# Splitting two-bank PSUM tiles, moving two kinds of copies from ScalarE to VectorE, and loading the first operands in smaller pieces: attention, a dense layer and routed experts on one Trainium2 core

## The chip, the core and the metric

The kernel runs on 1 core of one Trainium2 chip. The time is device microseconds of one execution. Three runs of the kernel before gave 766.39 us (median), 760.68 and 770.97 us. The rows shown below come from one profiled execution.

## What is computed

Everything is float32. Sizes: batch 4, 8 heads of width 64, 512 local and 32 global positions, 2304 tokens of width 512; 8 experts with hidden width 1024.

```python
# attention: a global row sees everything, a local row sees the globals and |i-j| <= 32
out_g = softmax(q_g @ [k_g, k_l].T / 8) @ [v_g, v_l]
out_l = softmax([q_l @ k_g.T, where(|i-j| <= 32, q_l @ k_l.T, -1e9)] / 8) @ [v_g, v_l]
x = concat(out_g, out_l)                      # 2304 x 512
# dense layer
h = x @ w_in                                  # 2304 x 2048
g = h if h >= 1, 0 if h <= -1, else (h + 1)**2 / 4
x = g @ w_out
# routed experts: tokens with x @ w_skip > 0 go to their best expert e
y = softmax(x @ w_gate)[e] * (relu(x @ w1[e]) @ w2[e])
out = x + y                                   # other tokens: out = x
```

## The kernel before, in words

The order of the instructions on every engine is the order of the program text; each engine works its queue off in order, and the framework puts in the waits, from which tile (a named buffer) an instruction reads or writes. Products that need float32 accuracy are done as three products of a high and a low part (`hi` = the value rounded to the matmul's own format, made by ScalarE; `lo` = the rest, by VectorE), so every weight and activation is split in two.

PSUM, the accumulator memory, has eight banks of 128 x 512 float32. `bank(i, name, shape)` (L81) gives a tile with the tag `b<i>`. Before the change the tags b0 and b6 hold tiles of two banks (`(128, 2, 512)`), b2 to b5 one bank each.

**Attention.** 32 steps (`for s in range(ND + 1)`, L440), one for each of 8 groups n (a batch element and half of its heads), two head pairs and two halves of the positions. In step s TensorE transposes the weights of step s (`transposes`, L302, results copied out by ScalarE at L309), makes the scores of a step up to three ahead (`scores`, L256, into an `s` tile; `take` at L208 alternates between two tiles of each kind), and the values of step s-1 (`values`, L319, L326). VectorE adds the mask and takes the maxima (L275), ScalarE does the exponentials (`exps`, L283), GpSimd scales by the reciprocal of the sum (L299) and copies the globals' columns (L315). VectorE copies the values out (L334).

Once per group, `globals_` (L220) does the same for the global rows in six pieces, divided by `yield`: four score matmuls into an `s` tile (L227); a maximum over 544 columns by VectorE (L230) and its multiple (L232); two exponentials by ScalarE (L234, L236); sum, reciprocal and scaling by VectorE (L239 to L244); two times four transposes (L250), each followed by a ScalarE copy to `pgT` (L252). Where the pieces run is written out by hand: `plan(g, ...)` (L409) names half-steps at which `between` (L413) advances the generator, and `mids` (L411, L454) advances it in a step, between that step's `scores` and `softmax`.

The weights `w_in` arrive as float64. `convert` (L88) makes the float32 value and its two parts in five pieces: load; two ScalarE scalings (L94 and L95); two VectorE bit operations (L97, L98); an add (L101); the high part by ScalarE (L104) and the low part by VectorE (L106). Eight of the 32 weight chunks are converted during attention (`plan(convert_in(...))`, L406), the others during the first 13 steps of the dense layer (`conversions`, L178).

**Dense layer.** Five units of up to 512 tokens, 16 steps each (`for m in range(NM)`, L757). A step is `stage1(m)` (L151: 12 matmuls at L158 into `h_ps[m % 2]`), `stage2(m - 1)` (L558: up to 12 matmuls at L565; in the last unit, which has 256 tokens, it trails by two steps), and `middle(m)` (L540), which turns h into g: ScalarE L544 and L545, VectorE L548 (the last reader of the h tile), ScalarE L549, VectorE L552. `h_ps` is the two halves of one two-bank tile `h` (L430). `route` (L489) works out the expert of every token, in five pieces.

**Experts.** Blocks of up to 256 tokens. `mm1(q, f)` (L702) makes one eighth of the hidden layer: 12 matmuls at L709 into `e_ps[f % 2]`, then ScalarE L713 and VectorE L714, its last reader. `e_ps` is the two halves of one two-bank tile `e` (L811). `mm2` (L740, L744) makes the output in the one-bank tiles `z0` and `z1`. In `products` (L877) a block with more than 128 tokens runs eight `mm1`, then `transpose_rows` (L696) of the next block's rows, then 16 `mm2`; `load_rows` (L685) gathers the next block's rows by indirect DMA on GpSimd's queue. A block of at most 128 tokens uses `mm1_few` (L720, L724), one `e` half after the other, and `transpose_few`. The first block is written out by itself (L813, L854): into its `mm1` the routing of the last two token tiles is woven (`hook`, L830), and after piece (6, 3) `choose_order` (L612), some 30 small VectorE instructions, after which the next rows can be looked up. During a block the next expert's weights are loaded (`prefetch`, L847) and split (L679, L680).

**Start.** SP issues the loads in this order (L364 to L371): half of K (400 KB), Q (512 KB), eight pieces of the mask (40 KB each), the other half of K, the identity, V.

Of the kernel before, what the change touches and what calls it, by code (L numbers as in the profile page):

```python
# [47 lines left out]
def tile_kernel(ctx, tc, q, k, v, w_in, w_out, wsg, w1, w2,  # L48
# [36 lines left out]

    def convert(raw, cvt, src, parts):  # L88
        flat = raw.rearrange("p a b -> p (a b)")
        low, high = raw[:, :, 0], raw[:, :, 1]  # L90
        nc.sync.dma_start(out=flat, in_=src.bitcast(I32))
        yield
        t = cvt() if callable(cvt) else cvt
        nc.scalar.activation(out=t.bitcast(F32), in_=high.bitcast(F32), func=AF.Copy, scale=2.0 ** -112)  # L94
        nc.scalar.activation(out=low, in_=low.bitcast(U32), func=AF.Copy, scale=2.0 ** -29)  # L95
        yield
        nc.vector.tensor_scalar(out=high, in0=high, scalar1=-(1 << 31), scalar2=None, op0=ALU.bitwise_and)  # L97
        nc.vector.scalar_tensor_tensor(out=t, in0=t, scalar=3, in1=high, op0=ALU.logical_shift_left,  # L98
                                       op1=ALU.bitwise_or)
        yield  # L100
        nc.vector.tensor_tensor(out=t, in0=t, in1=low, op=ALU.add)  # L101
        yield
        hi, lo = parts()
        nc.scalar.activation(out=hi, in_=t.bitcast(F32), func=AF.Copy)  # L104
        yield
        nc.vector.tensor_tensor(out=lo, in0=t.bitcast(F32), in1=hi.bitcast(F32), op=ALU.subtract)  # L106

    def convert_in(raw, t, f):
        return convert(raw, t, w_in[:, f, :], lambda: (winH[f], winL[f]))

    def convert_out(raw, t, f):
        def parts():
# [76 lines left out]
    with tc.tile_pool(name="att", bufs=1) as a1:  # L189
# [9 lines left out]
        P_a = [wp.tile([128, 2, 2, 2, 256], F32, tag=f"B{6 + i}", name=f"P_a{i}") for i in range(2)]  # L199
        P_b = [P_a[i // 2][:, i % 2] for i in range(4)]  # L200

        s_ps = [bank(6 * i, f"s{i}", (128, 2, 512)) for i in range(2)]
        t_ps = [bank(2 + i, f"t{i}", (128, 2, 2, 2, 64)) for i in range(2)]
        o_ps = [bank(4 + i, f"o{i}") for i in range(2)]
        turn = {"s": 0, "t": 0}
# [13 lines left out]

        def globals_(n):  # L220
            K = K_b[n % 2]
            g = take("s")
            for keys in (True, False):
                for i in range(2):
                    rhs = (K[:, i, 64:64 + NJ * W].rearrange("p (j c) -> p j c", c=W)[:, :, 0:128]
                           if keys else K[:, i, 32:64])
                    nc.tensor.matmul(g[64 * i:64 * i + 64, 0, :] if keys else g[64 * i:64 * i + 64, 1, 0:SG],  # L227
                                     lhsT=K[:, i, NSLOT:NK], rhs=rhs, start=True, stop=True)
            yield
            nc.vector.tensor_reduce(out=stg[:, 0:1], in_=g.rearrange("p b c -> p (b c)")[:, 0:512 + SG], axis=AX.X,  # L230
                                    op=ALU.max)
            nc.vector.tensor_scalar_mul(stg[:, 1:2], stg[:, 0:1], -0.125)  # L232
            yield
            nc.scalar.activation(out=Pg[:, :, 64:192], in_=g[:, 0].rearrange("p (j c) -> p j c", c=128),  # L234
                                 func=AF.Exp, bias=stg[:, 1:2], scale=0.125, accum_out=stg[:, 2:3])
            nc.scalar.activation(out=Pg[:, 0, 32:64], in_=g[:, 1, 0:SG],  # L236
                                 func=AF.Exp, bias=stg[:, 1:2], scale=0.125, accum_out=stg[:, 3:4])
            yield
            nc.vector.scalar_tensor_tensor(out=stg[:, 4:5], in0=stg[:, 2:3], scalar=1e-9, in1=stg[:, 3:4],  # L239
                                           op0=ALU.add, op1=ALU.add)  # L240
            nc.vector.reciprocal(out=stg[:, 5:6], in_=stg[:, 4:5])
            for j in range(NJ):
                x = Pg[:, j, (32 if j == 0 else 64):192]
                nc.vector.tensor_scalar_mul(x, x, stg[:, 5:6])  # L244
            yield
            for half in range(2):
                pt = take("t").rearrange("p h j a c -> p (h j a c)")
                for x in range(4):
                    j, t = 2 * half + x // 2, x % 2
                    nc.tensor.transpose(pt[:, 128 * x:128 * x + 128], Pg[:, j, 128 * t:128 * t + 128], ident)  # L250
                to = pgT[:, 2 * half:2 * half + 2].rearrange("p j t c -> p (j t c)")
                nc.scalar.activation(out=to, in_=pt, func=AF.Copy)  # L252
                yield


        def scores(s):  # L256
            n, i, jp = its[s]
            sp = s_of[s] = take("s")
            for a in range(2):
                for jj in range(2):  # L260
                    j = 2 * jp + jj
                    for h in range(2):
                        p = slice(64 * h, 64 * h + 64)
                        nc.tensor.matmul(sp[64 * jj:64 * jj + 64, h, 256 * a:256 * a + W], lhsT=Q_b[n % 2][p, i, j, :, a],
                                         rhs=K_b[n % 2][p, i, W * j + 96 * a:W * j + 96 * a + W], start=True, stop=True)

        def px(s, h, a):
            return P_b[s % 4][:, h, a, 96 * a:96 * a + W]
# [3 lines left out]
        def reduce_max(s, h, a):  # L272
            jp = its[s][2]
            m = 2 * a + (1 if jp == a else 0)
            nc.vector.tensor_tensor_reduce(  # L275
                out=px(s, h, a), in0=s_of[s][:, h, 256 * a:256 * a + W], in1=mask[:, m, :], scale=-0.125,
                scalar=3e38, op0=ALU.add, op1=ALU.min, accum_out=st_b[s % 4][:, 2 * h + a:2 * h + a + 1])

        def exps(s):
# [81 lines left out]
            yield  # L361
            nc.gpsimd.tensor_copy(out=tri, in_=trif)

        nc.sync.dma_start(out=K_b[0][:, 0], in_=k[0, :, 0])  # L364
        load(Q_b, q, 0)
        lo, up = slice(0, 64), slice(64, 128)
        for p, m, src in ((lo, 1, 1), (up, 1, 0), (lo, 0, 0), (up, 0, 0), (lo, 2, 2), (up, 2, 2), (lo, 3, 2), (up, 3, 3)):
            nc.sync.dma_start(out=mask[p, m], in_=c_mask[p, src])
        nc.sync.dma_start(out=K_b[0][:, 1], in_=k[0, :, 1])
        nc.sync.dma_start(out=ident, in_=c_ident)  # L370
        load(V_b, v, 0)  # L371
        nc.vector.memset(stg, 0.0)
        nc.scalar.activation(out=stg[:, 6:7], in_=stg[:, 7:8], func=AF.Exp)
        nc.gpsimd.memset(Pg, 0.0)
# [28 lines left out]
        for n in range(NG):  # L403
            o = 8 * n
            steps = {0: (0, 9, 11, 12, 13, 14), NG - 1: (-7, 0, 1, 2, 3, 4)}.get(n, (0, 5, 6, 7, 8, 9))
            plan(convert_in(raws[n % 2], cvts[n % 2], n), *(o + x for x in steps))  # L406
            if n + 1 < NG:
                g = globals_(n + 1)
                plan(g, o + 1, o + 1, o + 3)  # L409
                for x in (1, 2, 3):  # L410
                    mids[4 * n + x].append(g)  # L411
        plan(constants(), 2, 5, 6)
        def between(x):  # L413
            n, i8 = divmod(x, 8)
            for g in calls[x]:
                next(g, None)
            if i8 == 4 and 2 <= n < 6:
                split_x(0, [n - 2])

            if x == NS - 13:  # L420

                sp2 = wp.tile([128, 2, 512, 2], I32, tag="B2", name="sp2")
                sp2t = sp2[:, 1].rearrange("p a b -> p (a b)")[:, 0:512]
                sp0 = wp.tile([128, 2, 512, 2], I32, tag="B0", name="sp0")
                plan(convert_out(sp0[:, 0], cvts[0], 0), *(NS - y for y in (11, 7, 6, 5, 4, 3)))
                plan(convert_out(sp2[:, 0], sp2t, 1), *(NS - y for y in (12, 5, 4, 3, 2, 1)))
            if x == NS - 5:
                sp3 = wp.tile([128, 2, 512, 2], I32, tag="B3", name="sp3")
                raws.extend([sp3[:, 0], sp3[:, 1]])
                h2 = bank(0, "h", (128, 2, 512))  # L430
                h_ps.extend([h2[:, i] for i in range(2)])
                conversions(-2)
            if x == NS - 1:
                sp7 = wp.tile([128, 2, 512, 2], I32, tag="B7", name="sp7")
                raws.extend([sp7[:, 0], sp7[:, 1]])
                conversions(-1)
            if NS - 4 <= x < NS:
                stage1(0, [x - NS + 4])

        for s in range(ND + 1):  # L440
# [9 lines left out]
            for r in range(ahead, min(s + AHEAD + 1, ahead + 2, ND + 1)):  # L450
                if r < ND:
                    scores(r)
                if s < ND:
                    for g in mids[s]:  # L454
                        next(g)
                    mids[s] = []
                softmax(r, r - 1)
                if r < ND:
                    exps(r)
                ahead = r + 1  # L460
            if s >= 1:
                values(s - 1)
            if s < ND and i4 == 0 and 1 <= n and n + 1 < NG:
# [344 lines left out]
    hX = [[wp.tile([128, 2, BLK], F32R, tag=f"x{'hl'[hl]}{c}", name=f"h{hl}_{c}") for c in range(4)]  # L808
          for hl in range(2)]
    hH, hL = ([hX[hl][f // 2][:, f % 2, :] for f in range(NEF)] for hl in range(2))  # L810
    e2 = bank(0, "e", (128, 2, 512))  # L811
    e_ps = [e2[:, i] for i in range(2)]
    mm1(0, 0)  # L813
    stage2(NM - 1)
    store(4)
# [278 lines left out]
```

## Time and profile before

| | us |
|---|---|
| three runs: median, lowest, highest | 766.39, 760.68, 770.97 |
| the profiled execution, its own time | 762.76 |
| its span, first to last instruction | 761.1 |
| attention, until about | 142 |
| dense layer, about | 142 to 556 |
| first expert block, about | 554 to 595 |
| other expert blocks, about | 595 to 757 |

The span is what the trace shows; 1.7 us of the execution's own time lie around it. "Busy" is the time in which an engine has an instruction recorded. The engines are PE (TensorE's matmuls), PEld (its weight loads), DVE (VectorE), ACT (ScalarE), POOL (GpSimd) and SP (which only issues transfers). In a timeline or a group, the brackets or the last column name how long the engine sat idle before and which instruction ended that idle time. Ends of matmuls are modelled, so two matmuls in a row overlap in the records; their starts tell the pace.

### The profile page before, as it was taken

The page shows a single profiled execution, that of the slowest core. Times are in us where ns is not written, and L with a number is a line of the kernel's source. Part 1 is how long each engine was busy: PE and PEld are TensorE (multiplying, and loading weights), DVE is VectorE, ACT ScalarE, POOL GpSimd, SP SyncE. Part 2 cuts the span into 40 slices and gives each one's busy share as a digit, 9 for nine tenths or more (in the row PEclk, how much of TensorE's full clock was granted, in tenths as well). Part 3 has the DMA queues.
Part 4 walks back from the last instruction along what each step waited for, and adds up shares of the span by engine and source line. Part 5 has one row for each costly group of instructions (what it writes and reads, how often), then busy time and mean ns, then how long its engine had stood idle before and what let it go on. Part 6 is the DMA issues. An engine that isn't in the chain of part 4 may idle for free. (4 is left out here: it accounts for less than half of the span.)

```text
span 761.1 us, 12203 instructions
## 1 busy us (share of the span) xinstructions
PE 679.2 (89%) x4329; PEld 550.6 (72%) x4329; DVE 377.4 (50%) x1200; ACT 381.2 (50%) x903; POOL 134.3 (18%) x259
## 2 busy tenths in 40 slices
PE   5988888799999999999999999999976786879686
PEld 2666666588778777887778888887865675767574
DVE  3587677769994333243332444255644352222351
ACT  3899898768985333353333444466630241111241
POOL 1656454600000000000000010200022211202211
PEclk9999999999999999999999999999998999999999
DMA  7455443424511100011000231130012604101400
GB/s 271 163 188 217 186 182 139 167 83 139 169 53 42 70 1 1 0 71 42 1 1 1 110 112 56 29 112 29 1 56 82 211 29 152 50 7 57 151 18 23
DMA packets 21229, 66.06 MB, mean 87 GB/s; under 512 B 3675, under 2 KB 4829, under 8 KB 20116
## 3 DMA queue, kind: packets, MB, share of 16 engines
q1 hardware_dynamic: 18260, 58.41, 21.9%
q0 software_dynamic: 2880, 6.58, 2.9%
q8 instruction: 42, 0.69, 0.4%
q14 instruction: 47, 0.39, 0.2%
HBM read 54.95 MB, written 12.43 MB: 89 GB/s over the span
## 5 line engine op out<-in xcount | busy, mean ns | idle before, releaser
L565 PE MATMUL y<-wout,gh 128*128 128x512 f32 x544 | 140.0, 396 | 0.0
L158 PE MATMUL h<-xh,winH 128*128 128x512 f32 (+2 forms) x320 | 120.2, 376 | 7.7 <-DVE tb L548 7.3
L158 PE MATMUL h<-xh,winL 128*128 128x512 f32 (+2 forms) x320 | 115.4, 360 | 0.0
L158 PE MATMUL h<-xl,winH 128*128 128x512 f32 (+2 forms) x320 | 115.1, 360 | 0.0
L565 PEld LDWEIGHTS y<-wout,gh 128*128 128x128 f32 x544 | 99.4, 189 | 20.1 <-issue 1.2
L548 DVE SCALAR_TENSOR_TENSOR tb<-tb,h 128x512 f32<-128x512 f32 (+2 forms) x80 | 48.5, 606 | 119.1 <-ACT tb L545 118.7
L544 ACT ACTIVATE tb<-h,misc 128x512 f32<-128x512 f32 (+2 forms) x80 | 49.7, 622 | 95.1 <-PE h L158 81.3
L531 POOL DMA_INDIRECT table<-ids,slot x17 | 17.4, 1026 | 401.6 <-DVE slot L529 289.3
L709 PE MATMUL e<-yTH,WA 128*128 128x256 f32 x256 | 55.5, 298 | 31.4 <-DVE h L714 30.5
L158 PEld LDWEIGHTS h<-xh,winH 128*128 128x128 f32 x320 | 60.5, 189 | 24.4 <-DVE tb L548 15.7
L565 PE MATMUL y<-wout,gl 128*128 128x512 f32 x272 | 74.9, 390 | 0.0
L299 POOL TENSOR_SCALAR P_a<-P_a,st 128x160 f32<-128x160 f32 x128 | 59.3, 480 | 65.8 <-DVE st L295 57.9
L552 DVE TENSOR_TENSOR gl<-tb,gh 128x512 fp32r<-128x512 f32 (+2 forms) x80 | 48.9, 611 | 42.0 <-ACT gh L549 41.6
L709 PEld LDWEIGHTS e<-yTH,WA 128*128 128x128 f32 x256 | 42.9, 194 | 37.0 <-DVE h L714 35.7
L549 ACT ACTIVATE gh<-tb 128x512 fp32r<-128x512 f32 (+2 forms) x80 | 45.3, 567 | 45.2 <-DVE tb L548 45.2
L713 ACT ACTIVATE h<-e 128x256 fp32r<-128x256 f32 x40 | 15.3, 383 | 102.5 <-PE e L709 73.4
L158 PEld LDWEIGHTS h<-xh,winL 128*128 128x128 f32 x320 | 60.5, 189 | 8.0
L158 PEld LDWEIGHTS h<-xl,winH 128*128 128x128 f32 x320 | 60.6, 189 | 6.9
L565 PEld LDWEIGHTS y<-wout,gl 128*128 128x128 f32 x272 | 51.1, 188 | 11.0
L283 ACT ACTIVATE P_a<-P_a,st 128x160 f32<-128x160 f32 x128 | 53.1, 419 | 9.2 <-DVE st L275 9.1
L744 PE MATMUL z<-WA,h 128*128 128x512 f32 x240 | 57.6, 394 | 0.0
L744 PEld LDWEIGHTS z<-WA,h 128*128 128x128 f32 x240 | 44.6, 189 | 8.9
(208 smaller groups left out, 1086.4 us busy)
## 6 DMA issues: line engine op xcount, KB each, us to landing
xr<-in_w_dram SPq DMA_DIRECT2D x28, 512.0 KB, 6.6
V<-in_v_dram SPq DMA_DIRECT2D x8, 1024.0 KB, 7.6
K<-in_k_dram SPq DMA_DIRECT2D x7, 800.0 KB, 6.6
raw<-in_w_in_dram SPq DMA_DIRECT2D x10, 512.0 KB, 4.6
sp<-in_w_out_dram SPq DMA_DIRECT2D x10, 512.0 KB, 5.3
Q<-in_q_dram SPq DMA_DIRECT2D x8, 512.0 KB, 7.3
ys<-xT SPq DMA_DIRECT2D x15, 256.0 KB, 3.0
out_dram<-xT SPq DMA_DIRECT2D x15, 256.0 KB, 2.8
```

Of the source, the lines that this page charges most:

```text
L158: nc.tensor.matmul(hp, lhsT=lw, rhs=rx[:, 0:n], start=(c == 0 and k == 0), stop=(c == 3 and k == 2))
L283: nc.scalar.activation(out=px(s, h, a), in_=px(s, h, a), func=AF.Exp, bias=st[:, x:x + 1], scale=-1.0, accum_out=st[:, 4 + x:5 + x])
L299: nc.gpsimd.tensor_scalar(out=px(s, h, a), in0=px(s, h, a), scalar1=st[:, x:x + 1], scalar2=1.0, op0=ALU.mult, op1=ALU.mult)
L531: nc.gpsimd.indirect_dma_start(out=table[:, :], out_offset=bass.IndirectOffsetOnAxis(ap=slot[:, 0:1], axis=0), in_=ids[:, i, :], in_offset ...
L544: nc.scalar.activation(out=t, in_=hp, func=AF.Relu, bias=half, scale=0.5)
L548: nc.vector.scalar_tensor_tensor(out=t, in0=t, scalar=1.0, in1=hp, op0=ALU.min, op1=ALU.max)
L549: nc.scalar.activation(out=a, in_=t, func=AF.Copy)
L552: nc.vector.tensor_tensor(out=b_, in0=t, in1=a.bitcast(F32), op=ALU.subtract)
L565: nc.tensor.matmul(y_ps[q], lhsT=(gL if lows else gH)[:, s], rhs=wo(hl, f), start=(f == 0 and hl == 0 and not lows), stop=(f == NF - 1 and ...
L709: nc.tensor.matmul(hp, lhsT=lw, rhs=ry[:, c], start=(n == 0), stop=(n == 11))
L713: nc.scalar.activation(out=hH[f], in_=hp, func=AF.Relu)
L744: nc.tensor.matmul(z_ps[z], lhsT=lh[:, d], rhs=rw, start=(f == 0 and k == 0), stop=(f == NEF - 1 and k == 2))
```

## The change

- The `s0` pair, `h` and `e` tiles become two tiles of one bank each (tags b0 and b1). The second `s` buffer (b6) stays a two-bank tile.
- In `globals_`, the maximum becomes two reductions (512 and 32 columns) and one VectorE instruction that takes the larger and multiplies; the `pgT` copies move from ScalarE to VectorE.
- The six pieces of `globals_` are spread differently: the pieces at half-steps o+1, o+1, o+3 go to o+1, o+3, o+5, and the pieces in `mids` now run behind that step's `softmax` and `exps`.
- For the eight chunks converted during attention, the scaling of the high word (L94) moves from ScalarE to VectorE.
- The first loads: 416 of 800 columns of the first K half, then the whole mask in one piece, then the rest of K, all on SP; the first half of Q on ScalarE's queue, its second half behind V. Two rows of the mask that are equal to others but for a shift are copied by GpSimd.

```diff
-    def convert(raw, cvt, src, parts):
+    def convert(raw, cvt, src, parts, scale_on_vector=False):
...
-        nc.scalar.activation(out=t.bitcast(F32), in_=high.bitcast(F32), func=AF.Copy, scale=2.0 ** -112)
+        if scale_on_vector:
+            nc.vector.tensor_scalar_mul(t.bitcast(F32), high.bitcast(F32), 2.0 ** -112)
+        else:
+            nc.scalar.activation(out=t.bitcast(F32), in_=high.bitcast(F32), func=AF.Copy, scale=2.0 ** -112)
...
-        s_ps = [bank(6 * i, f"s{i}", (128, 2, 512)) for i in range(2)]
+        s6 = bank(6, "s6", (128, 2, 512))
+        s_ps = [[bank(i, f"s{i}") for i in range(2)], [s6[:, i] for i in range(2)]]
...
-            nc.vector.tensor_reduce(out=stg[:, 0:1], in_=g.rearrange("p b c -> p (b c)")[:, 0:512 + SG], axis=AX.X,
-                                    op=ALU.max)
-            nc.vector.tensor_scalar_mul(stg[:, 1:2], stg[:, 0:1], -0.125)
+            nc.vector.tensor_reduce(out=stg[:, 0:1], in_=g, axis=AX.X, op=ALU.max)
+            nc.vector.tensor_reduce(out=stg[:, 1:2], in_=g32[:, 0:SG], axis=AX.X, op=ALU.max)
+            nc.vector.tensor_scalar(out=stg[:, 1:2], in0=stg[:, 0:1], scalar1=stg[:, 1:2], scalar2=-0.125, op0=ALU.max,
+                                    op1=ALU.mult)
...
-                nc.scalar.activation(out=to, in_=pt, func=AF.Copy)
+                nc.vector.tensor_copy(out=to, in_=pt)
...
-        nc.sync.dma_start(out=K_b[0][:, 0], in_=k[0, :, 0])
-        load(Q_b, q, 0)
-        lo, up = slice(0, 64), slice(64, 128)
-        for p, m, src in ((lo, 1, 1), (up, 1, 0), (lo, 0, 0), (up, 0, 0), (lo, 2, 2), (up, 2, 2), (lo, 3, 2), (up, 3, 3)):
-            nc.sync.dma_start(out=mask[p, m], in_=c_mask[p, src])
+        first_keys = 2 * W + 96
+        nc.sync.dma_start(out=K_b[0][:, 0, 0:first_keys], in_=k[0, :, 0, 0:first_keys])
+        nc.scalar.dma_start(out=Q_b[0][:, 0], in_=q[0, :, 0])
+        nc.sync.dma_start(out=mask, in_=c_mask)
+        nc.sync.dma_start(out=K_b[0][:, 0, first_keys:NK], in_=k[0, :, 0, first_keys:NK])
         nc.sync.dma_start(out=K_b[0][:, 1], in_=k[0, :, 1])
         nc.sync.dma_start(out=ident, in_=c_ident)
         load(V_b, v, 0)
+        nc.sync.dma_start(out=Q_b[0][:, 1], in_=q[0, :, 1])
+
+        nc.gpsimd.tensor_copy(out=mask[64:128, 1], in_=mask[64:128, 0])
+        nc.gpsimd.tensor_copy(out=mask[0:64, 3], in_=mask[0:64, 2])
...
-            plan(convert_in(raws[n % 2], cvts[n % 2], n), *(o + x for x in steps))
+            plan(convert_in(raws[n % 2], cvts[n % 2], n, True), *(o + x for x in steps))
...
-                plan(g, o + 1, o + 1, o + 3)
+                plan(g, o + 1, o + 3, o + 5)
...
-                h2 = bank(0, "h", (128, 2, 512))
-                h_ps.extend([h2[:, i] for i in range(2)])
+                h_ps.extend([bank(i, f"h{i}") for i in range(2)])
...
-                if s < ND:
-                    for g in mids[s]:
-                        next(g)
-                    mids[s] = []
                 softmax(r, r - 1)
                 if r < ND:
                     exps(r)
                 ahead = r + 1
+            if s < ND:
+                for g in mids[s]:
+                    next(g)
...
-    e2 = bank(0, "e", (128, 2, 512))
-    e_ps = [e2[:, i] for i in range(2)]
+    e_ps = [bank(i, f"e{i}") for i in range(2)]
```

## Rows read from the trace of the kernel before

**Rows 1.** The page: busy time of each engine; granted TensorE clock in 40 slices, tenths.

```profile
PE 679.2 (89%) x4329; PEld 550.6 (72%) x4329; DVE 377.4 (50%) x1200; ACT 381.2 (50%) x903; POOL 134.3 (18%) x259
...
PEclk9999999999999999999999999999998999999999
```

**Rows 2.** Busy time by stretch: bounds, length, each engine's busy time, clock, DMA.

```profile
core 0: us, PE busy (x) PEld busy (x) DVE busy (x) ACT busy (x) POOL busy (x), PEclk, DMA share, GB/s
18.00:142.00 124.00, 108.68 (x1304) 83.25 (x1303) 87.95 (x428) 111.86 (x374) 71.46 (x183) 0.96 0.50 182
...
600.00:640.00 40.00, 30.35 (x190) 26.21 (x188) 17.85 (x33) 13.22 (x29) 6.61 (x9) 1.00 0.44 145
```

**Rows 3.** Waits over the whole span: waiter <- releaser: us in total, times, longest.

```profile
PEld e L709 <- DVE h L714: 46.3, 33, 6.2
...
PE e L709 <- DVE h L714: 39.6, 33, 6.1
...
PEld h L158 <- DVE tb L548: 15.7, 33, 2.7
...
PE t L250 <- ACT PT L309: 12.6, 13, 2.1
```

**Rows 4.** Timeline of one expert step: start us, us, instruction, count, idle before.

```profile
601.12 0.39 PE L709 MATMUL e<-yTH,WA 128*128 128x256 f32 x1 [0.93 <-DVE h L714]
...
602.53 0.28 PE L709 MATMUL e<-yTH,WA 128*128 128x256 f32 x1
...
603.27 0.42 DVE L714 SCALAR_TENSOR_TENSOR h<-e,h 128x256 fp32r<-128x256 f32 x1 [1.41 <-ACT h L713]
...
603.75 0.39 PE L709 MATMUL e<-yTH,WA 128*128 128x256 f32 x1 [0.93 <-DVE h L714]
```

**Rows 5.** Groups by line: shapes, count | busy us, mean ns | idle before, releasers.

```profile
L744 PE MATMUL z<-WA,h 128*128 128x512 f32 x240 | 57.6, 394 | 0.0
...
L252 ACT ACTIVATE pgT<-t 128x512 f32<-128x512 f32 x16 | 9.6, 598 | 4.0 <-PE t L250 4.0
...
L94 ACT ACTIVATE cvt<-raw 128x512 f32<-128x512 f32 x12 | 7.9, 657 | 0.0
...
L230 DVE TENSOR_REDUCE stg<-s 128x1 f32<-128x544 f32 x8 | 5.8, 723 | 6.3 <-PE s L227 6.3
...
L572 DVE COPY xT<-y 128x512 f32<-128x512 f32 x8 | 5.1, 681 | 0.0
```

**Rows 6.** Timeline around the end of the first expert block.

```profile
579.95 0.40 DVE L714 SCALAR_TENSOR_TENSOR h<-e,h 128x256 fp32r<-128x256 f32 x1
...
580.41 0.58 PE L709 MATMUL e<-yTH,WA 128*128 128x256 f32 x1 [6.12 <-DVE h L714]
...
583.51 1.01 POOL L687 DMA_INDIRECT nyg<-ys,nid  x1 [0.30 <-PE e L709]
...
593.12 0.59 PEld L698 LDWEIGHTS p<-ident,nyg 128*128 128x128 f32 x4
```

**Rows 7.** Transfers from 585 to 650 us: issues, count, median us to landing.

```profile
nyg<-ys,nid POOLq DMA_INDIRECT x4, 5.5
```

**Rows 8.** Timeline: the second expert's block, and a block of few rows.

```profile
694.49 0.50 PE L724 MATMUL e<-WA,yTH 128*128 128x512 f32 x1 [0.74 <-ACT hr L727]
...
709.17 0.69 DVE L889 COPY cyg<-nyg 128x1024 f32<-128x1024 f32 x1 [3.60 <-DMA out_dram<-ob,pid]
...
710.25 0.58 PE L709 MATMUL e<-yTH,WB 128*128 128x256 f32 x1 [3.52 <-DVE h L714]
```

**Rows 9.** Timeline of the start: first score matmuls, first matmuls of the globals.

```profile
6.04 1.34 PE L264 MATMUL s<-K,Q 64*64 64x160 f32 x16 [6.04 <-DMA Q<-in_q_dram]
...
10.46 2.13 PE L227 MATMUL s<-K 128*64 128x512 f32 x6 [1.18 <-DMA K<-in_k_dram]
```

**Rows 10.** Line 97 alone, ns min/median/max: up to 142 us, and from 160 to 235.

```profile
L97 DVE TENSOR_SCALAR raw<-raw x8: 426/477/509, 40.9 to 137.6; 128x512 int32<-128x512 int32 x8
...
L97 DVE TENSOR_SCALAR raw<-raw x8: 419/421/423, 166.2 to 227.2; 128x512 int32<-128x512 int32 x8
```

More of the change, by code (lines that the diff above doesn't have):

```diff
@@ L106, in convert, with convert_in @@
         nc.vector.tensor_tensor(out=lo, in0=t.bitcast(F32), in1=hi.bitcast(F32), op=ALU.subtract)
-    def convert_in(raw, t, f):
-        return convert(raw, t, w_in[:, f, :], lambda: (winH[f], winL[f]))
+    def convert_in(raw, t, f, scale_on_vector=False):
+        return convert(raw, t, w_in[:, f, :], lambda: (winH[f], winL[f]), scale_on_vector)
     def convert_out(raw, t, f):
@@ L221, in globals_ @@
             K = K_b[n % 2]
-            g = take("s")
+            g, g32 = take("s")
             for keys in (True, False):
@@ L226, in globals_ @@
                            if keys else K[:, i, 32:64])
-                    nc.tensor.matmul(g[64 * i:64 * i + 64, 0, :] if keys else g[64 * i:64 * i + 64, 1, 0:SG],
+                    nc.tensor.matmul(g[64 * i:64 * i + 64, :] if keys else g32[64 * i:64 * i + 64, 0:SG],
                                      lhsT=K[:, i, NSLOT:NK], rhs=rhs, start=True, stop=True)
             yield
-            nc.vector.tensor_reduce(out=stg[:, 0:1], in_=g.rearrange("p b c -> p (b c)")[:, 0:512 + SG], axis=AX.X,
-                                    op=ALU.max)
-            nc.vector.tensor_scalar_mul(stg[:, 1:2], stg[:, 0:1], -0.125)
+            nc.vector.tensor_reduce(out=stg[:, 0:1], in_=g, axis=AX.X, op=ALU.max)
+            nc.vector.tensor_reduce(out=stg[:, 1:2], in_=g32[:, 0:SG], axis=AX.X, op=ALU.max)
+            nc.vector.tensor_scalar(out=stg[:, 1:2], in0=stg[:, 0:1], scalar1=stg[:, 1:2], scalar2=-0.125, op0=ALU.max,
+                                    op1=ALU.mult)
             yield
-            nc.scalar.activation(out=Pg[:, :, 64:192], in_=g[:, 0].rearrange("p (j c) -> p j c", c=128),
+            nc.scalar.activation(out=Pg[:, :, 64:192], in_=g.rearrange("p (j c) -> p j c", c=128),
                                  func=AF.Exp, bias=stg[:, 1:2], scale=0.125, accum_out=stg[:, 2:3])
-            nc.scalar.activation(out=Pg[:, 0, 32:64], in_=g[:, 1, 0:SG],
+            nc.scalar.activation(out=Pg[:, 0, 32:64], in_=g32[:, 0:SG],
                                  func=AF.Exp, bias=stg[:, 1:2], scale=0.125, accum_out=stg[:, 3:4])
@@ L263, in scores @@
                         p = slice(64 * h, 64 * h + 64)
-                        nc.tensor.matmul(sp[64 * jj:64 * jj + 64, h, 256 * a:256 * a + W], lhsT=Q_b[n % 2][p, i, j, :, a],
+                        nc.tensor.matmul(sp[h][64 * jj:64 * jj + 64, 256 * a:256 * a + W], lhsT=Q_b[n % 2][p, i, j, :, a],
                                          rhs=K_b[n % 2][p, i, W * j + 96 * a:W * j + 96 * a + W], start=True, stop=True)
@@ L275, in reduce_max @@
             nc.vector.tensor_tensor_reduce(
-                out=px(s, h, a), in0=s_of[s][:, h, 256 * a:256 * a + W], in1=mask[:, m, :], scale=-0.125,
+                out=px(s, h, a), in0=s_of[s][h][:, 256 * a:256 * a + W], in1=mask[:, m, :], scale=-0.125,
                 scalar=3e38, op0=ALU.add, op1=ALU.min, accum_out=st_b[s % 4][:, 2 * h + a:2 * h + a + 1])
```

## The prediction

> **What bounds the kernel now.** I read the page's engine shares first: TensorE is busy 89% of the span and its clock is granted nearly everywhere, so only its idle time and what it waits for can be won [rows 1]. The busy time by stretch then parts the kernel. In attention it is ScalarE that has least room: 111.86 of 124.00 us, with TensorE at 108.68 and VectorE at 87.95. In the expert stretch no engine is full: TensorE 30.35 of 40.00 us, VectorE and ScalarE below half [rows 2]. There something makes TensorE wait, and the list of waits names it: 33 times the first matmul of `mm1` waits for VectorE's L714, 39.6 us in all. The same pattern, weaker, stands between the dense layer's L158 and L548: 15.7 us on the weight loads [rows 3].
>
> The timeline of one expert step shows why this wait looks needless. The matmuls that start at 603.75 write the half of `e` that was last read two pieces ago, yet they start only when the L714 that began at 603.27, which reads the other half, is done [rows 4]. `mm2` alternates between the one-bank tiles `z0` and `z1` in the same way and has no idle time before it at all [rows 5]. So the wait goes by tile, not by bank, and a one-bank tile should have it two pieces back.
>
> All sums are made against the profiled execution, 762.8 us (span 761.1 and 1.7 around it); the median of the three runs is 3.6 higher.
>
> **The experts' tiles.** A piece goes from 601.12 to 603.75: 2.63 us. Its twelve matmuls start within 601.12 to 602.53, and at that pace (0.118 us each when they run densely) twelve take 1.42. So a wait costs 1.20 us though only 0.93 is shown as idle: 0.27 more, since the tail of the last matmul and the exposed weight load count as busy [rows 4]. For 33 waits that is 39.6 + 33 x 0.27 = 48.5 us [rows 3]. Without the wait, piece f needs the L714 of piece f-2: the last matmul of f-2 starts 1.2 us before that L714 is over (602.53 to 603.27 + 0.42), one dense piece covers 1.42, so nothing is left in the steady part.
>
> What is late next, taken off:
> - First block. The 6.12 us before 580.41 is piece 7 waiting for an L714 queued behind `choose_order` [rows 6]. Piece 7 will run at once, then 20 products of `mm2` (512 columns, so about 0.236 each by the pace above) before the low part from that L714 is needed: 1.42 + 4.7 = 6.1 us of work for a wait of 6.12 + 0.27. What remains with the instruction itself I take as 1 us.
> - The gather for the next rows is issued at 583.51, its transposes run at 593.12, 9.6 us later [rows 6]. It hangs on `choose_order`, which moves forward only by the five or six waits ahead of it, while TensorE gains 5 us more: some 4.6 us are left for a landing that takes 5.5 in the median [rows 7]. 1 us.
> - Second expert's block: the L714 of its first piece is queued behind the copy L889, which starts at 709.17. TensorE now waits 3.52 us before piece 1; it will run piece 1 (1.42) and wait before piece 2 instead: 2.2 us remain [rows 8]. About 0.7 of the same kind in the block before.
>
> 48.5 - 5 = 43.5. In the two blocks of few rows, `mm1_few`'s second half waits 0.74 us for L727, which reads the first [rows 8]: 2 x (0.74 + 0.27) = 2.0. Together 45; bounds 25 (see the first rival) and 50.
>
> **The dense layer's tiles.** 33 waits, 15.7 us on the weight loads, the longest 2.7 [rows 3]. Next late is `stage2`, which needs the g of one step before and comes 12 matmuls after; in the last unit it trails by two steps. I take 12 us of the 15.7, as part of a weight load's idle time is covered by the matmul before; bounds 6 (half the steps find another wait) and 16.
>
> **Attention.** Off ScalarE inside the 18 to 142 us stretch: 14 copies L252 x 0.598 = 8.4 us and 8 scalings L94 x 0.657 = 5.3 us [rows 5]. Onto VectorE: 14 copies of 128x512 out of PSUM, by the nearest row L572 x 0.681 = 9.5; 8 scalings, between L97 in the same pattern (0.464 with POOL busy) and L94's own 0.657, I take 0.47: 3.8 [rows 5, 10]. The split maximum costs less than one of 0.723 per group twice over; by L230's pace I take 0.2 each, 1.6 in all (bounds 0 and 0.72 x 8 = 5.8) [rows 5]. So ScalarE goes from 111.9 to 98, VectorE from 88 to 103, TensorE stays at 108.7 [rows 2]. TensorE is then the longest, and at most 124 - 108.7 = 15 us can go. TensorE waits 12.6 us at the globals' transposes for ScalarE's L309, 13 times [rows 3]. The first four of each group move behind `values`, so half of that goes; the second four still follow the same step's L309. Against it: the `s` tile that the globals hold is given back half a step later, and between two `softmax` on VectorE there now stand normalising, scaling and a copy. With three engines within 10% of each other in fixed order, I take 6 us, bounds -6 and +13.
>
> A rule of the Trainium skill speaks against the moved scaling. First the row: L97, which reads and writes the same strided pattern, takes 0.477 us in the median beside a busy POOL and 0.421 where POOL has no work, 0.06 more [rows 10]. The skill ("SBUF — State Buffer", Who interferes with whom) says that a VectorE `tensor_scalar` may hold the port pair it shares with GpSimd for the whole instruction, the other fully blocking, while ScalarE never waits. Eight blocks of a whole GpSimd instruction would make some 3 us (an estimate from that page), the row only 0.5. I go by the row; the rest of the sum doesn't use this.
>
> **The start.** Ahead of the first scores 400 + 512 KB are asked for now; later 208 + 256 on two queues, the mask beside them. First scores at 6.04; in proportion to the bytes 3 us earlier. But the next stop is the second half of K, waited for until 10.46 [rows 9]: ahead of and with it 1632 KB now, 1376 later, in proportion 1.6 us earlier, and more because it is no longer issued behind eight mask loads. Then TensorE itself (1.34 of scores, the globals) is in the way. 2.5 us; bounds 0 (mask copies on POOL or a transfer on ScalarE's queue late) and 4.
>
> **Sum.** 45 + 12 + 6 + 2.5 = 65.5; 762.8 - 65.5 = 697.3. For runs that lie somewhat above the profiled execution, as here, I forecast 699 us; its own range is 685 to 713.
>
> **The rivals.**
> - *The next rows or weights bind the blocks.* Without stalls a block shrinks by some 8 us, but the gather still waits for the block's ids, and lands after 5.5 us [rows 7]. For it: the chain through POOL is as long as ever. Against: in the stretch 600 to 640 DMA is at 0.44 and all engines have room [rows 2]. If four blocks each lose 4 us and the first 4 more, 45 becomes 25: 719 us.
> - *VectorE becomes attention's bound.* Its 15 us come between the reductions that ScalarE waits for. For: 103 of 124 in fixed order. Against: TensorE still has more. Attention then loses 6 instead of winning 6: 711 us.
> - *The split does nothing*: the waits for L714 and L548 have another reason. Against it stands `z` [rows 5]. Without 45 and 12: 756 us.
> - *Slower: TensorE's clock in attention.* The clock was granted at 0.96 there [rows 2]. Should the new waits (for VectorE's copy out of the two transpose tiles) be long in every step, TensorE would run at the 1.2 GHz level instead of 2.4; all of its 108.7 us would then double. It decides from about 60 us of work at the low level, which eats all that the rest gains; at 75 us: 699 + 6 + 75 = 780. Against: in the worst stretch now the loss is a few per cent.
>
> **How the numbers follow.** Forecast 0.66, rows or weights 0.16, VectorE 0.12, no effect 0.04, clock 0.02. About 2% (15 us) can be told from no change. The first three are faster by more: 0.94; no effect lies within: 0.04; the clock is slower: 0.02. The range takes in the first two rivals and the bounds of attention and dense layer: 683 to 722.
>
> **What would show it.** Right: waits of L709 for L714 fall from 33 to a handful, one wide block's eight pieces take about 11.5 us; no wait of L158 for L548; TensorE busy over 95% in 600 to 640's work; attention shorter by some 6 us with ScalarE no longer fullest. Wrong: L709 waits for L714 as often as before, or transposes L698 wait for the gather, or attention gets longer with VectorE above 90%.

## The result and the profile after

| | before | after |
|---|---|---|
| median of four runs each, side by side (us) | 763.53 | 712.0 |
| lowest and highest | 759.88, 770.97 | 711.7, 716.04 |
| ratio, 95% interval | | 0.9326, 0.9241 to 0.941 |
| profiled execution, its span | 762.76, 761.1 | 711.86, 710.1 |
| first scores start | 6.04 | 4.60 |
| last value matmul starts | 149.6 | 156.9 |
| first expert matmul starts | 554.3 | 547.4 |

The last three rows cut the span into parts. The dense layer (from the last value matmul to the first expert matmul) went from 404.7 to 390.5 us: 14.2 gained. The experts (from there to the end) went from 206.8 to 162.7: 44.1 gained. Attention ends 7.3 us *later*, although it begins earlier. So the kernel is faster by about 51 us, and without attention it would have been more.

All line numbers from here on are those of the changed kernel: `mm1`'s matmul L717 and its last reader L722 (before L709, L714), dense L161 and L556 (L158, L548), scores L269 (L264), globals' transposes L255 (L250), their copy L257 (L252), the weights' copy L314 (L309), values L331 (L326).

The page's busy shares and granted clock, to be held against [rows 1]:

```profile
PE 665.7 (94%) x4329; PEld 547.3 (77%) x4329; DVE 389.9 (55%) x1232; ACT 371.6 (52%) x879; POOL 134.7 (19%) x261
...
PEclk9999999999999999999999999999999999999998
```

Busy time by stretch, as in [rows 2]: attention, the dense layer alone, and 40 us of the experts (bounds, length, PE, PEld, DVE, ACT, POOL, clock, DMA):

```profile
18.00:142.00 124.00, 102.42 (x1219) 76.92 (x1212) 92.53 (x435) 95.96 (x331) 65.42 (x173) 0.97 0.43 161
...
157.00:545.00 388.00, 387.94 (x1986) 321.09 (x1983) 203.02 (x535) 209.97 (x393) 18.14 (x18) 1.00 0.16 55
...
600.00:640.00 40.00, 40.00 (x277) 37.32 (x276) 13.24 (x28) 8.37 (x20) 8.83 (x10) 1.00 0.29 100
```

TensorE is now busy without a gap in the dense layer and in the expert stretch, where [rows 2] had 30.35 of 40 (the stretch is the same in time, not in work, as the blocks come earlier). In attention it does *less* in the same 124 us than before, 102.42 against 108.68, and no other engine has taken its place as the full one.

What L717 waited for, from the view of that one line (us, times). The view adds up matmuls and weight loads; [rows 3] had 39.6 us for the one and 46.3 for the other, 33 times each. Of the 1.0 us left, 0.3 are the matmuls':

```profile
  issue: 7.1, 8
  DVE h L722: 1.0, 3
```

The timeline of the first blocks, to be read against [rows 4] and [rows 6]: the end of the first block's `mm1`, the transposes of the gathered rows, three pieces of the next block by their last reader, and the two idle times of `mm1` at the start of the second expert's block, to be read against [rows 8].

```profile
568.24 4.60 PE L752 MATMUL z<-WA,h 128*128 128x512 f32 x19 [0.39 <-DVE h L722]
...
573.22 0.66 PE L706 MATMUL p<-ident,nyg 128*128 128x128 f32 x4 [0.39 <-DMA nyg<-ys,nid]
...
581.04 0.42 DVE L722 SCALAR_TENSOR_TENSOR h<-e,h 128x256 fp32r<-128x256 f32 x1 [0.23 <-ACT h L721]
...
582.48 0.42 DVE L722 SCALAR_TENSOR_TENSOR h<-e,h 128x256 fp32r<-128x256 f32 x1 [0.23 <-ACT h L721]
...
583.92 0.42 DVE L722 SCALAR_TENSOR_TENSOR h<-e,h 128x256 fp32r<-128x256 f32 x1 [0.23 <-ACT h L721]
...
663.85 0.28 PE L717 MATMUL e<-yTH,WB 128*128 128x256 f32 x1 [1.73 <-issue]
...
666.07 0.39 PE L717 MATMUL e<-yTH,WB 128*128 128x256 f32 x1 [0.27 <-DVE h L722]
```

A piece now comes every 1.44 us, where it took 2.63. L722 is no faster than L714 was: it just has a whole piece of time before its tile is written again. What was to be late next is late by 0.39 us in two of the places named, the end of the first block's `mm1` and the gather; in the second expert's block, where 2.2 us before piece 2 were foreseen, 0.27 are left there, and TensorE idles 1.73 us within piece 0, with no cause that the profile names.

### The profile page after: what moved, and what is told of

It is laid out like the page before. It is cut to its first block, busy times and chain, and to the rows that moved or that the text cites. A ratio compares the mean times of both kernels' runs of the same rounds, so it can differ in the third digit from the quotient of the medians.

```text
span 710.1 us, 12156 instructions
## 1 busy us (share of the span) xinstructions
PE 665.7 (94%) x4329; PEld 547.3 (77%) x4329; DVE 389.9 (55%) x1232; ACT 371.6 (52%) x879; POOL 134.7 (19%) x261
## 5 line engine op out<-in xcount | busy, mean ns | idle before, releaser
L161 PE MATMUL h<-xh,winH 128*128 128x512 f32 (+2 forms) x320 | 118.2, 369 | 0.0
L161 PE MATMUL h<-xh,winL 128*128 128x512 f32 (+2 forms) x320 | 114.6, 358 | 0.0
L161 PE MATMUL h<-xl,winH 128*128 128x512 f32 (+2 forms) x320 | 114.3, 357 | 0.0
L556 DVE SCALAR_TENSOR_TENSOR tb<-tb,h 128x512 f32<-128x512 f32 (+2 forms) x80 | 48.5, 607 | 105.4 <-ACT tb L553 104.9
L304 POOL TENSOR_SCALAR P_a<-P_a,st 128x160 f32<-128x160 f32 x128 | 60.5, 489 | 67.7 <-DVE st L300 61.4
L161 PEld LDWEIGHTS h<-xh,winH 128*128 128x128 f32 x320 | 60.2, 188 | 10.2 <-issue 2.1
L161 PEld LDWEIGHTS h<-xh,winL 128*128 128x128 f32 x320 | 60.2, 188 | 7.8
L161 PEld LDWEIGHTS h<-xl,winH 128*128 128x128 f32 x320 | 60.3, 189 | 7.3
L280 DVE CUSTOM_DVE_ANT_0 P_a<-s,mask 128x160 f32<-128x160 f32 x128 | 37.5, 314 | 27.3 <-PE s L269 18.9
L717 PE MATMUL e<-yTH,WA 128*128 128x256 f32 x256 | 48.7, 286 | 0.8 <-issue 0.7
L553 ACT ACTIVATE tb<-tb 128x512 f32<-128x512 f32 (+2 forms) x80 | 45.5, 568 | 2.5
```

The lines of the kernel that those rows point to most:

```text
L161: nc.tensor.matmul(hp, lhsT=lw, rhs=rx[:, 0:n], start=(c == 0 and k == 0), stop=(c == 3 and k == 2))
L280: nc.vector.tensor_tensor_reduce(out=px(s, h, a), in0=s_of[s][h][:, 256 * a:256 * a + W], in1=mask[:, m, :], scale=-0.125, scalar=3e38, op ...
L304: nc.gpsimd.tensor_scalar(out=px(s, h, a), in0=px(s, h, a), scalar1=st[:, x:x + 1], scalar2=1.0, op0=ALU.mult, op1=ALU.mult)
L553: nc.scalar.activation(out=t, in_=t, func=AF.Square)
L556: nc.vector.scalar_tensor_tensor(out=t, in0=t, scalar=1.0, in1=hp, op0=ALU.min, op1=ALU.max)
L717: nc.tensor.matmul(hp, lhsT=lw, rhs=ry[:, c], start=(n == 0), stop=(n == 11))
```

## Attention: the new wait

The list of waits between 18 and 150 us (waiter <- releaser: us in total, times, longest):

```profile
DVE P_a L280 <- PE s L269: 18.4, 17, 2.8
...
PEld t L255 <- ACT P_a L288: 12.6, 7, 2.3
...
PE t L255 <- DVE Pg L249: 10.8, 7, 2.0
DVE xl L142 <- ACT xh L141: 8.8, 4, 2.2
```

The old wait of the globals' transposes for ScalarE's copies, 12.6 us in [rows 3], is gone. In its place they wait for L249, VectorE's normalising of the globals' weights, once per group (the row of the weight loads, 12.6 us, is the same seven stalls). The timeline of one such step shows how that comes about:

```profile
57.39 0.69 DVE L234 TENSOR_REDUCE stg<-s 128x1 f32<-128x512 f32 x1
...
58.46 0.69 ACT L239 ACTIVATE Pg<-s,stg 128x512 f32<-128x512 f32 x1
...
59.29 1.04 PE L269 MATMUL s<-K,Q 64*64 64x160 f32 x16 [0.82 <-ACT Pg L239]
...
60.26 1.31 PE L331 MATMUL o<-PT,V 128*64 128x160 f32 x16
60.36 0.65 ACT L141 ACTIVATE xh<-xT 128x512 fp32r<-128x512 f32 x1
61.03 0.69 DVE L142 TENSOR_TENSOR xl<-xT,xh 128x512 fp32r<-128x512 f32 x1 [2.21 <-ACT xh L141]
61.64 0.32 DVE L280 CUSTOM_DVE_ANT_0 P_a<-s,mask 128x160 f32<-128x160 f32 x1
...
63.14 1.02 DVE L249 TENSOR_SCALAR Pg<-Pg,stg 128x160 f32<-128x160 f32 x4
...
63.59 0.63 PE L255 MATMUL t<-ident,Pg 128*128 128x128 f32 x4 [2.02 <-DVE Pg L249]
```

Read it from the end. The transposes at 63.59 wait 2.02 us for L249, which began at 63.14. L249 stands in VectorE's queue behind the whole `softmax` of its step (L280, from 61.64). That one is late twice over. Its scores could start only at 59.29, when the globals' exponential L239 had read the `s` tile that the globals held; they were done by 60.33. And ahead of it in VectorE's queue stands L142, the low part of a piece of the dense layer's input, which waits 2.21 us for its high part: L141 is in ScalarE's queue behind the same exponential and the weights' copies L314, and runs from 60.36. `softmax` starts as L142 ends.

L142 runs in four of the groups only. In these four the transposes wait 2.02 us each for L249; in the other three they wait 0.89 to 0.93, as here, one group earlier:

```profile
45.58 0.63 PE L255 MATMUL t<-ident,Pg 128*128 128x128 f32 x4 [0.93 <-DVE Pg L249]
```

While all this runs, the next values wait: they start at 67.05, as the starts of the value matmuls in the group of the step at 59.29 show:

```profile
49.03 1.31 PE L331 MATMUL o<-PT,V 128*64 128x160 f32 x16
52.23 1.31 PE L331 MATMUL o<-PT,V 128*64 128x160 f32 x16
56.14 1.31 PE L331 MATMUL o<-PT,V 128*64 128x160 f32 x16
...
67.05 1.31 PE L331 MATMUL o<-PT,V 128*64 128x160 f32 x16
```

The four steps take 18.02 us (49.03 to 67.05; the start at 60.26 is in the timeline above). The same group before:

```profile
49.48 1.31 PE L326 MATMUL o<-PT,V 128*64 128x160 f32 x16
...
60.31 1.31 PE L326 MATMUL o<-PT,V 128*64 128x160 f32 x16
65.66 1.31 PE L326 MATMUL o<-PT,V 128*64 128x160 f32 x16
```

That is 16.18. The last of the four steps took 5.35 (60.31 to 65.66) and takes 6.79 now. Reckoned from the start of each group's last value matmuls to the next group's, which gives 16.18 and 17.8 here, four of the seven groups grew by 1.6 us each, the four with L142; of the other three one grew by 1.1 and two by nothing. With 2.1 us in the first group that is 9.7 us, against 2.4 won at the start.

## The experiments

Two theories stood after that. *Spacing*: the new half-steps put normalising directly ahead of its transposes, with only a step's values between, and let the globals hold an `s` tile longer. *VectorE*: the copies and scalings moved there are what makes everything late. The first four runs part them. Ratios are to the kernel before on the same chip (median 764.99 us in the first four runs, 765.92 in the second four). The changed kernel itself was timed only beside the 763.53 of the first table; differences to it are between medians of separate comparisons.

**plan_back**: the changed kernel with one line put back.

```diff
-                plan(g, o + 1, o + 3, o + 5)
+                plan(g, o + 1, o + 1, o + 3)
```

> The changed kernel with one line undone: the pieces of globals_ run at half-steps o+1, o+1, o+3 again (still behind softmax), so normalising comes half a step earlier than the transposes that need it. Theory S (the new spacing costs attention its time: TensorE waits for L249, 10.8 us, and for the globals' exponentials, 8.2 us, in the changed kernel's trace): 701 to 704 us, the wait of L255 for L249 below 2 us in all. Rival V (VectorE has too much to do because of the copies and scalings): 709 to 712 us.

Measured: 702.38 us, ratio 0.9193 (0.9124 to 0.9263), 9.6 us below the changed kernel by the medians (the two intervals overlap by 0.002, the runs' ranges lie 8 us apart); in the profiled execution the last value matmul starts at 146.5, 10.4 us earlier. Its waits in attention:

```profile
ACT P_a L288 <- DVE st L280: 16.8, 22, 1.8
DVE stg L244 <- ACT Pg L241: 12.1, 7, 1.9
...
DVE P_a L280 <- PE s L269: 5.3, 10, 1.2
```

L255 no longer waits for L249 at all, L142 no longer for L141, and `softmax` waits 5.3 us for its scores instead of 18.4. The pieces meet their data: VectorE waits for the exponentials' sums (L244) where TensorE used to wait for VectorE. One line explains what attention lost. Some 3 of the 10.4 us are two falls of the granted clock, which this execution does not have (last section); the line moves maximum, exponentials and normalising at once, and no run parts them.

**copy_back**: the changed kernel with the `pgT` copies on ScalarE again.

```diff
-                nc.vector.tensor_copy(out=to, in_=pt)
+                nc.scalar.activation(out=to, in_=pt, func=AF.Copy)
```

> The changed kernel with the pgT copies on ScalarE again, everything else as changed. Theory S: 710 to 714 us, the waits of L255 for L249 stay. Rival V: 703 to 706 us, VectorE's 9 us less on the path.

Measured: 720.46 us, ratio 0.9434 (0.9364 to 0.9505): 8 us *slower* than the changed kernel by the medians, with intervals that overlap a little, and above both theories' ranges. The profiled executions differ by 5.8 us: 2.2 lie in attention (last value matmul 159.1), 3.6 in the experts, whose code is the same; why those are longer stays open.

```profile
DVE P_a L280 <- PE s L269: 28.0, 21, 2.0
...
PE t L255 <- DVE Pg L249: 10.8, 7, 2.0
```

The new wait is the same to the tenth. Taking the copies off VectorE makes attention no shorter, so their move is not what made it longer; with the new spacing it is rather worth those 2.2 us.

**scale_back**: the changed kernel with the eight scalings on ScalarE again.

```diff
-            plan(convert_in(raws[n % 2], cvts[n % 2], n, True), *(o + x for x in steps))
+            plan(convert_in(raws[n % 2], cvts[n % 2], n), *(o + x for x in steps))
```

> The changed kernel with the scaling of the high word on ScalarE again in attention. Theory S: 710 to 714 us. Rival V: 708 to 710 us, by the 3.5 us of VectorE's work.

Measured: 710.8 us, ratio 0.9305 (0.9236 to 0.9374), 1.2 us below the changed kernel and inside its interval. The wait for L249 stays at 10.8 us. With copy_back this ends the VectorE theory: neither move, put back, makes the kernel faster by what that theory asked.

**tiles_only**: the kernel before with nothing but the one-bank tiles and the split maximum that they need.

```diff
-        s_ps = [bank(6 * i, f"s{i}", (128, 2, 512)) for i in range(2)]
+        s6 = bank(6, "s6", (128, 2, 512))
+        s_ps = [[bank(i, f"s{i}") for i in range(2)], [s6[:, i] for i in range(2)]]
...
-                h2 = bank(0, "h", (128, 2, 512))
-                h_ps.extend([h2[:, i] for i in range(2)])
+                h_ps.extend([bank(i, f"h{i}") for i in range(2)])
...
-    e2 = bank(0, "e", (128, 2, 512))
-    e_ps = [e2[:, i] for i in range(2)]
+    e_ps = [bank(i, f"e{i}") for i in range(2)]
```

> The kernel before with nothing but the one-bank tiles (s0 pair, h, e, and the split maximum that the tiles need). If the dense layer and the experts gained by the tiles alone (14.1 and 44.1 us between the traces) and attention lost by the rest: 58 us less than before, 704 to 706 us, attention ending within 1 us of before. If attention's loss came from the split tiles or the second maximum: 711 to 715 us.

Measured: 703.31 us, ratio 0.9197 (0.9127 to 0.9268). This is a little below the 704 to 706 expected of the tiles. They alone are worth 61.7 us; everything else in the change takes back 8.7. In attention the wait of [rows 3] is there as before (this kernel's L252 and L311 are L250 and L309), though the last value matmul comes 2.7 us earlier than in the kernel before, some 1.5 of them one fall of the clock less. In the second expert's block piece 2 waits as the prediction has it:

```profile
PE t L252 <- ACT PT L311: 12.2, 12, 2.0
...
656.95 0.39 PE L710 MATMUL e<-yTH,WB 128*128 128x256 f32 x1 [2.20 <-DVE h L715]
```

The next four runs ask what the remaining parts are worth once the spacing is right, and whether a better kernel than both can be had.

**sched_back**: the changed kernel with the whole old order of the globals' pieces: plan_back's line, and the pieces in `mids` ahead of `softmax` again.

```diff
-                plan(g, o + 1, o + 3, o + 5)
+                plan(g, o + 1, o + 1, o + 3)
...
+                if s < ND:
+                    for g in mids[s]:
+                        next(g)
+                    mids[s] = []
                 softmax(r, r - 1)
...
-            if s < ND:
-                for g in mids[s]:
-                    next(g)
```

> The changed kernel with the whole old schedule of globals_ (half-steps o+1, o+1, o+3, and the other pieces between scores and softmax again); the copies and the scaling stay on VectorE. If only the spacing of the pieces cost time: 701 to 704 us, as with the half-steps alone put back (702.4). If running them behind softmax is worth something by itself (the copies on VectorE then stand ahead of the reductions that ScalarE waits for): 705 to 710 us.

Measured: 698.26 us, ratio 0.912 (0.9024 to 0.9216), wholly below the changed kernel's interval: 13.7 us by the medians, and below both ranges expected. Its waits, and its busy time in the stretch of [rows 2], come from two views:

```profile
ACT P_a L288 <- DVE st L280: 22.1, 15, 2.1
...
PE t L255 <- ACT PT L314: 13.1, 14, 2.2
```

```profile
18.00:142.00 124.00, 108.63 (x1311) 82.29 (x1304) 102.64 (x461) 100.46 (x353) 78.62 (x187) 0.99 0.49 178
```

With the order undisturbed, ScalarE has lost 11.4 us and VectorE has taken 14.7 (against 111.86 and 87.95 before), and yet TensorE waits as long for L314 as it did for L309. A group takes 16.28 us, as before the change.

**tiles_start**: tiles_only with the new first loads.

```diff
-        nc.sync.dma_start(out=K_b[0][:, 0], in_=k[0, :, 0])
-        load(Q_b, q, 0)
...
+        first_keys = 2 * W + 96
+        nc.sync.dma_start(out=K_b[0][:, 0, 0:first_keys], in_=k[0, :, 0, 0:first_keys])
+        nc.scalar.dma_start(out=Q_b[0][:, 0], in_=q[0, :, 0])
...
```

> The kernel before with the one-bank tiles and the new first loads, attention's schedule and copies as before. The first loads brought step 2's scores 2.6 us earlier in the changed kernel's trace. If that carries through: 700 to 701.5 us against 703.3 with the tiles alone. If attention takes it back because ScalarE is its bound: 703 us. Against 702.4 with all of the change but the half-steps, this also says what the moved copies and the scaling are worth: nothing if 702, a loss if below.

Measured: 700.72 us, ratio 0.9131 (0.9037 to 0.9225), 2.6 us below tiles_only by the medians, with intervals that overlap. It differs from sched_back by the copies and scalings alone, which stay on ScalarE here: 700.72 against 698.26, no difference that these runs can tell. In the profiled executions attention even ends 3.4 us earlier here (the last value matmul starts at 143.3 against 146.7); what puts sched_back's execution ahead lies in the experts, whose code is the same (159.6 against 164.3 us).

**norm_late**: the changed kernel with the plan of plan_back, but normalising one half-step later than there: still ahead of its step's `softmax`, and with more time for the globals' exponentials that it needs.

```diff
-                plan(g, o + 1, o + 3, o + 5)
+                plan(g, o + 1, o + 1, o + 4)
```

> The changed kernel with the half-steps o+1, o+1, o+4: matrix products and maximum in one go as before the change, the normalising one half-step later than before it. With o+3 VectorE waits 12.1 us there for the globals' exponentials (L244 for L241). If that wait is on the path: 694 to 699 us. If VectorE would have waited for the next scores anyway: 701 to 703 us.

Measured: 702.38 us, ratio 0.9172 (0.9089 to 0.9255): the same as plan_back. What is left at the transposes is a wait of the weight loads, and some 1 us of the matmuls':

```profile
DVE stg L244 <- ACT Pg L241: 8.7, 6, 1.5
...
PEld t L255 <- ACT PT L314: 4.9, 13, 0.8
```

So both waits at L255, the old one for L314 and the new one for L249, can be all but removed, and the time does not fall below that of sched_back, which keeps 13.1 us of one of them.

**all_banks**: norm_late with the other two-bank tiles split too (the second `s` buffer, the routing's and the small blocks' tiles).

```diff
-        s6 = bank(6, "s6", (128, 2, 512))
-        s_ps = [[bank(i, f"s{i}") for i in range(2)], [s6[:, i] for i in range(2)]]
+        s_ps = [[bank(i, f"s{i}") for i in (6 * k, 6 * k + 1)] for k in range(2)]
...
-    r_ps = bank(6, "r", (128, 2, 512))
+    r_ps = [bank(6 + i, f"r{i}") for i in range(2)]
...
-    f_ps = bank(6, "f", (128, 2, 4, 128))
+    f_ps = [bank(6 + i, f"f{i}", (128, 4, 128)) for i in range(2)]
```

> As the kernel with o+1, o+1, o+4, and the three other two-bank tiles (the second s buffer, r of the routing, f of the short blocks) in one-bank tiles too. If every two-bank tile costs waits like e and h did: 2 to 5 us less than that kernel, above all in the routing steps of the first expert block and the last unit. If these tiles were never waited for across banks: within 1 us of it.

Measured: 701.05 us, ratio 0.9151 (0.9067 to 0.9234), not to be told from norm_late. Of the tiles split here only the `s` buffer showed a wait that went by the tile, and a small one: the scores' wait for the globals' exponentials goes from 7.7 to 6.8 us. Splitting paid where a long wait went by the tile.

## Why the prediction was right, and where it was wrong

The time forecast was 699 us; 712.0 lies in the range and at the upper edge of the likeliest case's own. The 13 us between are one term: attention came out 15.7 us worse than forecast, outside its own bounds of -6 and +13, and the other three terms together 1.2 better. That the total still lay in the range is the range's width, which took in the rivals, and not this term.

- **Experts: 45 predicted, 44.1 measured.** The wait is by tile, it goes with the split, and a piece falls from 2.63 to 1.44 us where 1.42 was worked out. Of the 5 us that were to stay, the 1 us at the first block and the 1 us at the gather came out at 0.39 each, while the 2.2 before piece 2 of the second expert's block came as foreseen in tiles_only (2.2) and tiles_start (2.1); the changed kernel has 1.73 us within piece 0 and 0.27 there. One wait was not foreseen: 3.0 us at 689.79, before a block of few rows, ended by VectorE's sequencer at the branch L961, where the kernel before and sched_back have 1.0 and every other run 3.0 to 3.3; its cause stays open. Sums of this size carry some 3 us of noise either way: in the profiled executions of the kernels above, whose expert code is the same, this part takes 159.6 us (sched_back) to 166.3 (copy_back, tiles_only).
- **Dense layer: 12 predicted, 14.2 measured.** Of the 33 waits of [rows 3] one is left, 0.2 us. `stage2` was not late next: TensorE is busy 387.94 of 388 us. Nearly all of the 15.7 us came back, so the discount for what the matmul before covers was too large.
- **Start: 2.5 predicted.** The value matmuls begin 2.4 us earlier; tiles_start gives 2.6 by the medians, within the noise. The size is right, a link is not: the first scores come 1.4 us earlier, not the 3 that the bytes gave. The new wait of VectorE for the mask's copies on GpSimd, foreseen as a bound, is there and costs next to nothing: the first `softmax` starts 1.51 us after the first scores (6.11 and 4.60), against 1.40 before (7.44 and 6.04).
- **Attention: 6 gained predicted, 9.7 lost measured.** This is the step that failed: "With three engines within 10% of each other in fixed order, I take 6 us". It weighed engines' totals, and those came out: VectorE at 102.64 where 103 was worked out, ScalarE at 100.46 where 98 was, in sched_back. Neither mattered. In every run with the old spacing, tiles_only and tiles_start with the copies on ScalarE, sched_back with them on VectorE, the group that took 16.18 us before takes 16.2 to 16.3. Moving a copy from one engine to another gave a group nothing there. What does change its length is the order in the queues: 17.8 with the new half-steps, 16.9 and 16.2 in turn in plan_back, 16.7 and 16.1 in norm_late. That a group is as long as its chain from score to softmax to exponentials to transposes to values fits this; no run shows it by itself. The text named the two causes, the `s` tile that "is given back half a step later" and normalising between two `softmax`, set no price on either, and counted the 12.6 us of waits for L309 as half won. They were all won, and 10.8 us for L249 came in their place. What it did not look at is L141 and L142, which the later exponentials hold up and `softmax` queues behind: the four groups that hold them are the four that grew by 1.6 us.
- **The rivals.** *VectorE becomes attention's bound*, at 711, names nearly the time that came, by another cause, so this hit is luck: VectorE has 31 of 124 us idle, and taking work off it makes nothing better by more than the 1.2 us of scale_back, which these runs can't tell from nothing (copy_back is slower). That VectorE is in fixed order, as the rival says, is part of what happened; that it has too much to do is not. *Rows or weights bind the blocks* fell: the gather's wait is 0.39 us. *The split does nothing* fell with tiles_only. *Clock*: below.
- **The skill's rule on the shared port.** Moved to VectorE, the scaling L95 takes 436 ns in the median of eight and 595 at the longest, where 470 was taken from [rows 10]. (L97 was a near row, not the same form: L95 reads the same strided words but writes a packed tile.) The longest is 172 ns above the shortest, 423; none shows a wait as long as a GpSimd instruction, the shortest L304 taking 387. So the row was the better guide than the rule of the Trainium skill ("SBUF — State Buffer", Who interferes with whom) that one of the two engines blocks for the other's whole instruction, and in scale_back the whole move makes no difference that these runs can tell.

What stays open: which link of attention's chain sets the 16.2 us of a group. Removing the waits at L255 (norm_late) and unloading ScalarE (sched_back) both left it there. Open too is how the 1.6 us of a group part between L142 and the rest: no run moves L142 alone.

## What to carry to other kernels

When a matmul waits for a reader of the *other* half of its tile, look at how the buffer is declared: the split alone gave 61.7 of 765 us. When a stage has no full engine, don't price a moved copy by the engines' totals; follow one period of the loop from its last instruction back, and ask of each moved piece what now stands ahead of it in its queue. Undo a bundled change part by part: one line of it cost 9.6 us, and the kernel with the lowest median here (sched_back, 698.26 us) is the change without its reordering, though tiles_start, all_banks and norm_late, at 700.72 to 702.38, can't be told from it.

## What the chip showed that was not expected

Groups of attention come in two lengths that differ by 1.5 us, in the kernel before and after alike: 16.18 and 17.66 before, 17.8 and 19.26 after. The longer ones hold a short fall of the granted clock. Before, by stretches of 1 us (clock is the third figure from the end):

```profile
80.00:81.00 1.00, 0.00 (x0) 0.00 (x0) 0.92 (x2) 1.00 (x4) 0.68 (x3) 1.00 0.00 0
81.00:82.00 1.00, 0.90 (x8) 0.71 (x10) 1.00 (x9) 0.67 (x3) 0.00 (x0) 0.88 0.00 0
82.00:83.00 1.00, 1.00 (x10) 0.93 (x8) 0.97 (x6) 1.00 (x4) 0.68 (x1) 0.50 0.00 0
83.00:84.00 1.00, 1.00 (x9) 0.52 (x7) 0.00 (x0) 1.00 (x6) 1.00 (x4) 0.50 0.00 0
84.00:85.00 1.00, 1.00 (x7) 1.00 (x6) 0.49 (x1) 0.10 (x2) 0.82 (x3) 0.50 0.00 0
85.00:86.00 1.00, 1.00 (x17) 0.83 (x19) 0.00 (x0) 0.80 (x2) 0.00 (x0) 0.91 0.00 0
```

TensorE had stood idle for 1.72 us before 81.10, and then its clock fell to 0.50, the 1.2 GHz level, from 81.75 until about 85.25. In the timeline the sixteen value matmuls take 2.37 us instead of 1.31:

```profile
81.10 0.66 PE L250 MATMUL t<-ident,Pg 128*128 128x128 f32 x4 [1.72 <-ACT PT L309]
81.69 2.37 PE L326 MATMUL o<-PT,V 128*64 128x160 f32 x16
```

The same wait of 1.72 us at 65.07, one group earlier, brought no fall: the value matmuls behind it, at 65.66, take 1.31 (shown above). And tiles_start has the same wait in the same place and keeps its clock:

```profile
77.98 0.66 PE L252 MATMUL t<-ident,Pg 128*128 128x128 f32 x4 [1.73 <-ACT PT L311]
78.57 1.31 PE L328 MATMUL o<-PT,V 128*64 128x160 f32 x16
```

So an idle time of this length may or may not bring the fall, and each fall costs 1.5 us of a group. Seen in the profiled executions, there are two such long groups before and after, one in tiles_only and sched_back, and none in plan_back, norm_late and tiles_start. The value matmuls of tiles_start end 3.6 us before those of tiles_only, 2.0 of that from the start. The clock rival's mechanism is seen here; its size is a few us of 700.
